# A retention-attention and gMLP kernel: per-chunk states formed for two chunks at once and summed in SBUF, four rotating PSUM banks, zero products in the head, a new order

## The chip, the cores and the metric

The kernel runs on one core of one Trainium2 chip. The metric is device time in microseconds (us) of the whole program: loads, arithmetic and stores. The core has a tensor engine (PE), a vector engine (DVE), a scalar engine (ACT), a general engine (POOL) and a queue engine (SP) that issues nearly all DMAs. Each of them works through its own list of instructions in order and waits on semaphores for the others.

## The reference

Inputs q, k, v have 8 batches, 8 heads, 576 positions and 64 elements in f32. A retention attention feeds a gated MLP that also mixes along the sequence:

```python
scores = scale * q @ k^T                       # per batch and head
ret    = scores * gamma[h] ** (s - t)          # 0 for t > s
x      = (ret @ v), heads side by side         # [8, 576, 512]
h      = gelu_tanh(x @ w_in)                   # [8, 576, 1024]
u, vv  = halves of h
v_n    = (vv - mean) / sqrt(var + 1e-6) * g_ln
v_s    = w_sg @ v_n + b_sg                     # along the 576 positions
out    = x + (u * v_s) @ w_out
```

## The kernel before

The 8 x 576 = 4608 positions are cut into 36 chunks of 128; two neighbouring chunks form a block, so there are 18 blocks of 256 positions. Nine chunks hold two batches, and the fifth chunk of each nine (index 4, called MID) holds the end of one batch and the start of the next.

Attention is done chunk by chunk: inside a chunk by masked scores, across chunks by a state, the running sum of k-transposed times v over all earlier chunks of the batch. The decay goes into factors on q and v, so the state is a plain sum. For block j the steps are: `ld` (loads q, k, v by SP), `cast` (to bf16, with the decay factors; on POOL, DVE or ACT), `T` and `Te` (PE transposes q and k, an engine copies the result to SBUF) or `Td` (a DMA transposes), `Sc` and `Sce` (scores of four heads, DVE multiplies by the mask), `Z` and `Ze` (state products of one chunk, copy of the state as bf16 `zb`), `inter` (state times q for one half), `intra` (masked scores times v, and the rest of the state products), `intrae` (copy of the attention to `xT`). The MLP follows with `V`, `Ve`, `mom`, `pow`, `cen`, `norm` (the v half of w_in, gelu, layer norm), `U`, `Ue` (the u half), `W`, `We` (w_sg along the sequence, times u) and `O`, `Oe`, `st` (w_out, copy, store). `wT` transposes w_sg once at the start.

The order of all these steps, and for many the engine (A, D or P for ACT, DVE, POOL) and the PSUM bank, is written out by hand in one string, `ORDER`. The program takes the words in turn, so the string sets each engine's list.

PSUM has eight banks. Tag `y` holds the scores (two banks), tag `z` the attention or V (two), `x0`, `x1` and `w` one bank each, which T, wT, U, W and O share in turn. The eighth bank belongs to the state alone: `Z` of every chunk adds into it, over a whole batch, and `Ze` reads it after each chunk:

```python
z = zcur[0]                                     # one bank, kept over the chunks of a batch
nc.tensor.matmul(z[half(r), kk, :], s["kb"][lo, a, kk, r, :], s["vb"][lo, a, h, :],
                 start=(first and r not in begun), stop=True, skip_group_check=True)
```

`Z` of chunk c uses the 64 rows of that chunk (32 for MID), so its 16 products lie on one half of PE's rows, on two column halves in turn.

Of the kernel before, what the change touches and what calls it, by code (L numbers as in the profile page):

```python
# [32 lines left out]
mom:3:1 ld:6:k:0 We:0:0:0 Z:5:0 Sce:5:0 Ze:5:0:A Ve:4:b W:0:3:0:2:w cast:6:q:P ld:7:q wc:out:A W:0:1:1:2:x1 ld:6:v:0 We:0:3:0 W:0:2:0:2:x0 We:0:2:0
inter:5 We:0:1:1 Sc:5:1 W:0:1:0:2:w W:0:2:1:2:x0 W:0:3:1:2:x1 Sce:5:1 We:0:2:1 We:0:1:0 intra:5 cast:6:k:P pow:2:1 Z:5:1 We:0:3:1 ld:7:k intrae:5:A
U:4:1:w T:6:q:x0 V:5:b:z cen:3:0 Ue:4:1 Ze:5:1:A cen:3:1 cast:7:q:P T:6:k:x1 mom:4:0 U:5:1:w ld:7:v Te:6:q:A W:0:0:1:0:x0 Te:6:k:A U:5:0:x1 Sc:6:0
norm:2:1:P cast:6:v:D mom:4:1 Z:6:0 Ve:5:b W:0:0:1:1 cast:7:k:P Ue:5:1 O:0:0:w We:0:0:1 Sce:6:0 mom:5:0 pow:3:b Ue:5:0 Ze:6:0:A O:1:1:x0 Z:6:1 inter:6
norm:3:0:D ld:8:q cast:7:v:P Td:7:q Oe:1:1:A Sc:6:1 Sce:6:1 ld:8:k Oe:0:0:A O:0:1:x0 norm:3:1:A T:7:k:x1 ld:8:v cen:4:1 mom:5:1 Ze:6:1:A Te:7:k:A
U:4:0:w bd:1 ld:9:q intra:6 Ue:4:0 Sc:7:0 pow:4:b intrae:6:A Z:7:0 Oe:0:1:A ld:9:k O:1:0:x1 cen:5:1 cen:4:0 ld:10:k Sce:7:0 V:6:b:z Ze:7:0:D
cast:8:k:A Ve:6:b cast:8:q:P pow:5:b Oe:1:0:A U:6:1:x0 norm:4:0:D T:8:k:w inter:7 Te:8:k:D Sc:7:1 cast:8:v:P Z:7:1 Sce:7:1 T:8:q:x1 Ue:6:1 cen:5:0
st:0 Ze:7:1:A W:1:3:0:2:w ld:9:v W:1:2:0:2:x0 Te:8:q:A We:1:2:0 intra:7 Sc:8:0 cast:9:k:P Z:8:0 norm:4:1:A Td:9:k W:1:0:1:2:x1 We:1:3:0 W:1:0:0:2:w  # L40
ld:11:k:0 W:1:1:0:2:x0 mom:6:0 We:1:0:1 norm:5:0:A We:1:0:0 intrae:7:A U:7:0:x1 Ue:7:0 V:7:b:z We:1:1:0 Ve:7:b O:2:1:x1 mom:6:1 cast:10:k:P ld:10:q
Oe:2:1:A Ze:8:0:D Sce:8:0 cast:9:q:P ld:11:q:0 mom:7:0 cast:9:v:P ld:10:v W:1:3:1:2:w inter:8 Sc:8:1 We:1:3:1 norm:5:1:P ld:11:q:1 Sce:8:1 mom:7:1
T:9:q:x1 U:6:0:w W:1:1:1:2:x0 We:1:1:1 Te:9:q:A Z:9:0 Ue:6:0 cen:6:1 cen:6:0 intra:8 intrae:8:A Sc:9:0 pow:6:b W:1:2:1:2:x1 norm:6:0:D cast:10:q:P
U:7:1:w V:8:b:z norm:6:1:A W:2:3:0:2:x0 pow:7:b Ue:7:1 Td:10:k We:1:2:1 Sce:9:0 ld:11:k:1 Ve:8:b Ze:9:0:A ld:11:v:1 cen:7:0 W:2:0:0:2:x1 U:8:1:w
cast:10:v:P We:2:3:0 Z:9:1 inter:9 Sc:9:1 Ue:8:1 mom:8:0 W:2:0:1:2:x0 T:10:q:w ld:13:k:1 We:2:0:0 Sce:9:1 norm:7:0:A Te:10:q:D W:2:3:1:2:x1 Ze:9:1:A
intra:9 st:1 Sc:10:0 Z:10:0 W:2:1:1:2:w We:2:3:1 We:2:0:1 Ze:10:0:A O:3:0:x1 intrae:9:A mom:8:1 cast:11:q:P ld:11:v:0 pow:8:b Sce:10:0 cast:11:k:A
We:2:1:1 cen:7:1 O:3:1:x0 V:9:b:z cen:8:1 Td:11:q U:8:0:w Oe:3:1:A Oe:3:0:A cen:8:0 Ve:9:b W:2:2:1:2:x1 norm:7:1:A mom:9:0 norm:8:0:P inter:10 Z:10:1
Sc:10:1 Ue:8:0 We:2:2:1 Ze:10:1:A O:2:0:x0 Oe:2:0:A W:2:2:0:2:x1 Sce:10:1 norm:8:1:P Td:11:k W:3:0:1:2:w W:2:1:0:2:x0 ld:12:q ld:13:q:0 intra:10
Sc:11:0 ld:12:k We:2:2:0 We:3:0:1 We:2:1:0 intrae:10:A st:3 ld:12:v cast:11:v:P Z:11:0 W:3:0:0:2:w W:3:3:0:2:x0 Sce:11:0 cast:12:q:P V:10:b:z We:3:0:0
cast:12:k:P Td:12:k W:3:2:0:2:w Ve:10:b We:3:3:0 ld:13:v:1 cast:12:v:P Ze:11:0:D U:9:0:x0 Ue:9:0 We:3:2:0 T:12:q:x1 Z:11:1 inter:11 Sc:11:1 Ze:11:1:A  # L50
mom:9:1 Te:12:q:D O:5:1:w ld:13:k:0 W:3:2:1:2:x1 pow:9:b Sce:11:1 We:3:2:1 U:10:1:x0 intra:11 Oe:5:1:A Z:12:0 cen:9:0 cen:9:1 Sc:12:0 Ue:10:1
intrae:11:A O:5:0:x0 mom:10:0 ld:13:q:1 cast:13:k:A norm:9:0:P Sce:12:0 Oe:5:0:A cast:13:q:P V:11:b:z ld:14:k mom:10:1 Ve:11:b W:3:1:0:2:x1 st:2
U:9:1:w Ze:12:0:A mom:11:0 Ue:9:1 pow:10:b Td:13:k We:3:1:0 O:4:0:x0 cen:10:0 inter:12 Sc:12:1 Oe:4:0:A norm:9:1:A Sce:12:1 U:11:1:w T:13:q:x1
cen:11:0 Te:13:q:A W:3:1:1:2:x0 intra:12 We:3:1:1 st:5 Z:12:1 ld:14:q cast:14:k:P Ue:11:1 Sc:13:0 mom:11:1 O:4:1:x1 U:11:0:w ld:15:k:1 cen:10:1
intrae:12:A U:10:0:x0 V:12:b:z Oe:4:1:A cast:14:q:D O:7:0:x1 pow:11:b ld:13:v:0 Ze:12:1:A ld:14:v Sce:13:0 Ue:11:0 ld:15:q:0 U:12:0:w Ue:10:0
norm:10:0:P Td:14:q U:12:1:x0 norm:10:1:D norm:11:0:A Ve:12:b Ue:12:0 cast:13:v:P W:4:2:1:2:w Oe:7:0:D Td:14:k ld:15:q:1 mom:12:0 cen:11:1 We:4:2:1
Ue:12:1 W:4:3:1:2:x1 We:4:3:1 inter:13 norm:11:1:P cast:14:v:P Z:13:1 Sc:13:1 W:4:2:0:2:w st:4 mom:12:1 W:4:0:1:2:x0 Ze:13:1:A ld:15:v:0 We:4:2:0
# [35 lines left out]
def kernel(  # L93
# [274 lines left out]
    def Z_mm(j, c):  # L368
# [4 lines left out]
        if first:  # L373
            zcur[0] = psZ.tile([128, KK, D], F32, name="zp")
# [229 lines left out]
```

## Time and profile before

| | |
|---|---|
| median of 3 runs | 219.21 us (219.15 to 220.51) |
| profiled execution | 218.48 us, span 216.7 us |
| PE busy | 194.7 us (90%) |
| DVE busy | 170.3 us (79%) |
| ACT busy | 123.3 us (57%) |
| POOL busy | 122.1 us (56%) |
| DMA | 48.47 MB, mean 224 GB/s |

The span is the time from the first to the last record of the profiled execution; what is missing to its own time, 1.78 us, lies around the span. Busy times are sums over the engine's records. A row of a timeline has start, length, engine, line, operation, tiles and count, and in brackets the idle time before it with what ended it. A group row of the page has count, busy time and mean of one in ns.

### The profile page before, as it was taken

The numbers are of one execution on the slowest core, as the hardware profiler recorded it, in microseconds if no ns is written. First come the engines' busy times: TensorE is split into PE (matmuls) and PEld (weight loads), VectorE is DVE, ScalarE is ACT, GpSimd is POOL, SyncE is SP. The second block draws the span as 40 slices with busy tenths as digits, with TensorE's granted clock in tenths as the row PEclk, the third lists the DMA queues.
The fourth block names the chain that finished last, engine by engine and source line by source line (L and its number), as shares of the span: only waits on it lengthen the run. The fifth ranks groups of instructions, "written<-read, shape, count | busy, mean of one in ns | idle before, by whom it ended". The sixth has DMA issues, their size and how long they took to land.

```text
span 216.7 us, 7228 instructions
## 1 busy us (share of the span) xinstructions
PE 194.7 (90%) x3101; PEld 136.8 (63%) x3130; DVE 170.3 (79%) x289; ACT 123.3 (57%) x179; POOL 122.1 (56%) x144
## 2 busy tenths in 40 slices
PE   0468788899999989999999999999999999999993
PEld 0355566577677657686667767686756675666751
DVE  3666858988995899799977678797988887977770
ACT  3356475697868578567563477833674457633102
POOL 5055338889169996988368565659729422151000
PEclk9999999999999999999999999999999999999999
DMA  6999999998999999999779899999899999450755
GB/s 168 290 343 355 222 233 263 208 226 190 290 217 254 208 247 324 197 249 174 184 172 282 180 263 252 217 207 254 128 269 230 265 238 271 141 149 3 191 198 194
DMA packets 86704, 48.47 MB, mean 224 GB/s; under 512 B 24528, under 2 KB 79824, under 8 KB 86672
## 3 DMA queue, kind: packets, MB, share of 16 engines
q1 hardware_dynamic: 86560, 48.00, 96.7%
q8 instruction: 24, 0.39, 0.8%
q14 instruction: 8, 0.07, 0.1%
q10 hardware_dynamic: 112, 0.00, 0.0%
HBM read 33.05 MB, written 9.44 MB: 196 GB/s over the span
## 4 chain that ended last, share of the span: by engine, by line
PE 63%; DVE 16%; DMA 12%; ACT 2%; issue 2%; SPq 1%; POOL 1%; DVEq 0%; ACTq 0%; POOLq 0%
PE wp L523 14%; PE op L535 12%; DMA vf<-in_v_dram 12%; PE hv L454 11%; PE hu L509 10%; PE ot L419 5%; DVE ret L360 5%; PE sc L350 3%; DVE vc L484 3%; PE zp L382 2%; DVE bst L468 2%; PE op L538 2%; DVE vn L500 2%; PE wtp L279 2%; PE tp L327 2%
## 5 line engine op out<-in xcount | busy, mean ns | idle before, releaser
L360 DVE TENSOR_TENSOR ret<-sc,mask 128x1024 bf16<-128x1024 f32 x36 | 43.8, 1216 | 5.8 <-PE sc L350 5.6
L302 POOL TENSOR_TENSOR qb<-qf,gq 128x512 bf16<-128x512 f32 x30 | 32.7, 1109 | 22.1 <-DMA qf<-in_q_dram 20.7
L523 PE MATMUL wp<-wT,vn 128*128 128x288 bf16 x256 | 40.8, 286 | 0.1
L509 PE MATMUL hu<-xT,w_in 128*128 128x256 bf16 x288 | 36.8, 273 | 0.0
L535 PE MATMUL op<-w_out,gT 128*128 128x512 bf16 x126 | 35.0, 380 | 1.2 <-issue 0.3
L528 DVE TENSOR_TENSOR gT<-wp,uT 128x288 bf16<-128x288 f32 x64 | 28.0, 449 | 9.8 <-PE wp L523 8.2
L454 PE MATMUL hv<-w_in,xT 128*128 128x512 bf16 x133 | 34.0, 382 | 1.6 <-ACT xT L137 0.8
L137 ACT CAST xT<-ot 128x1024 bf16<-128x1024 f32 x17 | 22.3, 1311 | 17.8 <-PE ot L419 17.7
L484 DVE SCALAR_TENSOR_TENSOR vc<-vg,mv,g_bc 128x512 f32<-128x512 f32 x36 | 31.5, 897 | 0.2
L514 ACT ACTIVATE uT<-hu 128x512 bf16<-128x512 f32 x36 | 21.3, 599 | 16.7 <-PE hu L509 16.4
L509 PEld LDWEIGHTS <-w_in 128*128 128x128 bf16 x288 | 27.1, 98 | 5.0
L523 PEld LDWEIGHTS <-vn 128*128 128x128 bf16 x256 | 24.6, 98 | 8.0 <-issue 0.4
L309 POOL TENSOR_TENSOR vb<-vf,gv 128x1024 bf16<-128x1024 f32 x13 | 25.1, 1934 | 7.2 <-DMA vf<-in_v_dram 5.5
L468 DVE BATCH_NORM_STATS2 bst<-vg 128x6 f32<-128x512 f32 x36 | 24.6, 683 | 4.5 <-ACT vg L461 4.5
L461 ACT ACTIVATE vg<-hv 128x1024 f32<-128x1024 f32 (+1 forms) x19 | 18.6, 980 | 13.2 <-PE hv L454 11.6
L500 POOL TENSOR_SCALAR vn<-vc,rs 128x512 bf16<-128x512 f32 x12 | 20.6, 1720 | 9.3 <-DVE vc L484 9.2
L454 PEld LDWEIGHTS <-xT 128*128 128x128 bf16 x144 | 13.5, 99 | 14.7 <-ACT xT L137 1.4
L137 ACT COPY ob<-op 128x512 f32<-128x512 f32 x20 | 11.5, 586 | 18.5 <-PE op L538 17.8
L477 POOL TENSOR_SCALAR rs<-mv 128x2 f32<-128x2 f32 (+1 forms) x19 | 8.1, 427 | 23.8 <-DVE mv L469 22.8
L535 PEld LDWEIGHTS <-gT 128*128 128x128 bf16 x144 | 12.9, 98 | 11.6
L523 PE MATMUL wp<-wT,vnm 128*128 128x288 bf16 x64 | 18.0, 287 | 0.3 <-DVE kT L137 0.3
L350 PE MATMUL sc<-qT,kT 64*64 64x128 bf16 x576 | 16.3, 223 | 0.8 <-DVE ret L360 0.6
(74 smaller groups left out, 283.2 us busy)
## 6 DMA issues: line engine op xcount, KB each, us to landing
out_dram<-ob SPq DMA_DIRECT2D x16, 512.0 KB, 4.6
kf<-in_k_dram SPq DMA_DIRECT2D x12, 512.0 KB, 7.6
qf<-in_q_dram SPq DMA_DIRECT2D x12, 512.0 KB, 6.6
vf<-in_v_dram SPq DMA_DIRECT2D x12, 512.0 KB, 8.1
gT<-in_moe_w_in_dram SPq DMA_DIRECT2D x2, 1024.0 KB, 9.5
qf<-in_q_dram SPq DMA_DIRECT2D x4, 384.0 KB, 8.2
kf<-in_k_dram SPq DMA_DIRECT2D x4, 384.0 KB, 8.3
vf<-in_v_dram SPq DMA_DIRECT2D x4, 384.0 KB, 8.5
```

What stands on the lines that cost most here:

```text
L137: (nc.scalar.copy if eng == "A" else ENG[eng].tensor_copy)(o, i)
L302: ENG[eng].tensor_tensor(s["qb"][:, a], paired(x)[:, a], g, op=Alu.mult)
L309: ENG[eng].tensor_tensor(s["vb"][:].rearrange("p a h d -> p h a d"), x[:], bc(gv, j), op=Alu.mult)
L360: nc.vector.tensor_tensor(s["ret"][:, :, 2 * g:2 * g + 2].rearrange("p r x a t -> p r x (a t)"), PS.pop(("Sc", j, g))[:].rearrange("p r x ...
L454: nc.tensor.matmul(hv[:, n], xT[:, (2 * j + t) % (2 * RING), kk, :], w_in[:, kk, F2:], start=(kk == 0), stop=(kk == KK - 1))
L468: nc.vector.bn_stats(bst[:], s["vg"][:, t])
L484: nc.vector.scalar_tensor_tensor(s["vc"][:, t], s["vg"][:, t], s["mv"][:, t, 0:1], g_bc[:], op0=Alu.subtract, op1=Alu.mult)
L500: ENG[eng].tensor_scalar(vn[:], vc[:, t], rs[:, t:t + 1], None, op0=Alu.mult)
L509: nc.tensor.matmul(hu[:, i, :], w_in[:, kk, 128 * c:128 * c + 128], xT[:, c0:c0 + 2, kk, :], start=(kk == 0), stop=(kk == KK - 1), skip_gr ...
L523: nc.tensor.matmul(PS["W", b, c, x][:], vns[t0 + j][e][:, 128 * c:128 * c + 128], wT[:, e, j, x * HS:(x + 1) * HS], start=(j == 0), stop=( ...
L528: nc.vector.tensor_tensor(gT[:, c, col:col + HS], PS.pop(("W", b, c, x))[:], uT[:, c, col:col + HS], op=Alu.mult)
L535: nc.tensor.matmul(op[:], gT[:, c, 128 * i:128 * i + 128], w_out[:, c, :], start=(c == 0), stop=(c == KK - 1 and not turn), skip_group_che ...
```

## The change

Five things change; the arithmetic of the rest, the layer norm among it, stays.

- `Z` of a block issues the products of both its chunks in one group, alternating between the two halves of PE's rows, each chunk into a bank of its own. Blocks with a MID chunk run the two chunks one after the other, and the last chunk of two batches needs no state. The state's own bank is gone; there are now four rotating banks, `x0`, `x1`, `w`, `v`, for Z too.
- `Ze` adds the bank to the running sum of the batch in SBUF, in f32 (DVE), or copies it where a batch starts. A new step `Zc` casts that sum to bf16 (19 on ACT, 10 on POOL, 3 on DVE).
- A step `fill` issues products of zeros (128 columns by 512) on PE: 32 of them in eleven places up to the first V group of block 1.
- The 64 last rows of w_sg are staged in the gT ring (`s5`) instead of a tile of their own, and some tables of the set-up share buffers with later tiles.
- `ORDER` is written anew. Block 2's loads and attention stand ahead of the loads of the u half of w_in and of w_sg; the transposes of w_sg stand after block 2; many casts and copies change engines.

```diff
-zcur = [None]
-def Z_mm(j, c):
...
-    if first:
-        zcur[0] = psZ.tile([128, KK, D], F32, name="zp")
...
+def opens(i):
+    return i % NT in (0, MID)
+
+def Z_mm(j, c, tag):
+    s = blk[j]
+    PS["Z", j, c] = ps2("zp", [128, KK, D], tag)
+    if c == 0 and (2 * j + 1) % NT != NT - 1:
+        return
+    for part in (False, True):
+        rows = [[], []]
+        for c in range(2):
+            if ("Z", j, c) not in PS or ((2 * j + c) % NT == MID) != part:
+                continue
+            lo = slice(64 * c + (32 if part else 0), 64 * c + 64)
+            for a in range(2):
+                for kk in range(KK):
+                    for r in range(2):
+                        rows[c].append((r, 64, lambda z=PS["Z", j, c], lo=lo, a=a, kk=kk, r=r: nc.tensor.matmul(
+                            z[half(r), kk, :], s["kb"][lo, a, kk, r, :], s["vb"][lo, a, hd(r, kk), :],
+                            start=(a == 0 and kk == 0), stop=True, skip_group_check=True)))
+        interleave(rows)
 
 def Z_out(j, c, eng):
-    zb = zbs[2 * j + c + 1] = w3.tile([128, KK, D], BF, name="zb")
-    move(eng, zb[:], PS.pop(("Z", j, c))[:])
+    i = 2 * j + c
+    sums[i] = w2.tile([128, KK, D], F32, name="zs")
+    z = PS.pop(("Z", j, c))
+    if opens(i):
+        move(eng, sums[i][:], z[:])
+    else:
+        nc.vector.tensor_tensor(sums[i][:], z[:], sums[i - 1][:], op=Alu.add)
+
+def Z_cast(j, c, eng):
+    i = 2 * j + c
+    zbs[i + 1] = w3.tile([128, KK, D], BF, name="zb")
+    move(eng, zbs[i + 1][:], sums[i][:])
...
+def fill(n, tag):
+    o = ps2("idle", [128, 4, 128], tag)
+    for _ in range(n):
+        nc.tensor.matmul(o[:], zeros[:], zeros[:].unsqueeze(1).to_broadcast([128, 4, 128]), start=True, stop=True,
+                         skip_group_check=True)
...
-    wst5 = consts.tile([64, S], F32, name="wst5")
+    ..., "s5": flat[:64, :S]}
```

Of the string, its first words:

```diff
-ld:0:k rl ld:0:q ld:0:v cast:0:k:D ld:1:k T:0:k:x1 ld:1:q mk:0 cast:0:q:D Te:0:k:A T:0:q:x1 cast:0:v:D Z:0:0 ...
+ld:0:q warm rl mk:0 ld:0:k ld:0:v cast:0:q:P fill:10:v T:0:q:v ld:1:q cast:0:k:P ld:1:k fill:2:w T:0:k:w ldw:v ...
```

What this makes of the engines' lists is shown at three places. First DVE at the start of block 0; before, it casts k (`kb`) and scales q (`qb`) itself:

```order
L137 CAST kb<-kf 128x512 x2
L246 TENSOR_SCALAR mask_136<-rel 128x256
L302 TENSOR_TENSOR qb<-qf,gq 128x512 x2
L309 TENSOR_TENSOR vb<-vf,gv 128x8x2x64
L246 TENSOR_SCALAR mask_137<-rel 128x256
L249 MEMSET mask_137 32x4x16
L360 TENSOR_TENSOR ret<-sc,mask_136 128x2x512
```

And of the change, where `zs` is the sum of the states in SBUF:

```order
L259 TENSOR_SCALAR mask_134<-rel 128x256
L322 TENSOR_TENSOR vb<-vf,gv 128x8x2x64
L259 TENSOR_SCALAR mask_136<-rel 128x256
L262 MEMSET mask_136 32x4x16
L140 COPY zs<-zp 128x256
L373 TENSOR_TENSOR ret<-sc,mask_134 128x2x512
```

The casts of k and q of block 0 have moved to POOL, and the copy of the first state now stands on DVE between v's scaling and the first masking (`ret`).

Second, PE at the state products of block 1. Before, with buffer numbers, at the first of them, behind the scores (`sc`):

```order
L350 LDWEIGHTS kT_335
L350 MATMUL sc_350<-qT_322,kT_335 64x128
L382 LDWEIGHTS kb_239
L382 MATMUL zp_181<-vb_369,kb_239 64x64
```

And of the change, behind the V group (`hv`):

```order
L477 LDWEIGHTS xT_87
L477 MATMUL hv_363<-w_in_85,xT_87 128x512
L398 LDWEIGHTS kb_344
L398 MATMUL zp_381<-vb_358,kb_344 64x64
L398 LDWEIGHTS kb_344
L398 MATMUL zp_384<-vb_358,kb_344 64x64
```

Before, all 16 products go on into `zp_181`, the one bank; now 32 products take the banks `zp_381` and `zp_384` in turn.

Third, DVE in the middle of the program, around block 5's and block 6's states. Of the change:

```order
L506 SCALAR_TENSOR_TENSOR vc<-vg,mv,g_bc 128x512
L550 TENSOR_TENSOR gT<-wp,uT 128x288 x2
L413 TENSOR_TENSOR zs<-zp,zs 128x256 x2
L373 TENSOR_TENSOR ret<-sc,mask_134 128x2x512
L550 TENSOR_TENSOR gT<-wp,uT 128x288
L373 TENSOR_TENSOR ret<-sc,mask_134 128x2x512
L322 TENSOR_TENSOR vb<-vf,gv 128x8x2x64
L506 SCALAR_TENSOR_TENSOR vc<-vg,mv,g_bc 128x512
L413 TENSOR_TENSOR zs<-zp,zs 128x256
```

The three additions into `zs` stand ahead of the masking of scores there; before, the states of these chunks were copied to `zb` by ACT and no row of DVE stood in their place.

160 lines of the change are left out of this document (75 added, 85 removed).

## Prediction

> **What bounds the kernel now.** I read the page first: engine shares, slices, the chain that ended last.
>
> ```profile
> PE 194.7 (90%) x3101; PEld 136.8 (63%) x3130; DVE 170.3 (79%) x289; ACT 123.3 (57%) x179; POOL 122.1 (56%) x144
> ...
> PE   0468788899999989999999999999999999999993
> ...
> PE 63%; DVE 16%; DMA 12%; ACT 2%; issue 2%; SPq 1%; POOL 1%; DVEq 0%; ACTq 0%; POOLq 0%
> ```
>
> PE carries 63% of the chain and its row of slices is full from the ninth slice on. Then I asked for busy time by stage, cut at the ends of the attention of blocks 1, 5 and 9 and at PE's last instruction.
>
> ```profile
> core 0: us, PE busy (x) PEld busy (x) DVE busy (x) ACT busy (x) POOL busy (x), PEclk, DMA share, GB/s
> 0.00:24.60 24.60, 11.80 (x256) 8.81 (x258) 14.57 (x30) 12.38 (x16) 9.11 (x32) 1.00 0.99 283
> 24.60:63.20 38.60, 36.06 (x663) 25.90 (x667) 33.16 (x57) 26.89 (x39) 26.11 (x28) 1.00 1.09 230
> 63.20:105.10 41.90, 40.03 (x707) 29.44 (x709) 37.37 (x56) 28.22 (x41) 35.77 (x37) 1.00 1.14 241
> 105.10:212.90 107.80, 106.64 (x1500) 72.64 (x1514) 85.24 (x150) 55.27 (x82) 51.12 (x48) 1.00 0.89 203
> 212.90:216.70 3.80, 0.14 (x3) 0.00 (x0) 0.00 (x0) 0.59 (x1) 0.00 (x0) 1.00 0.44 168
> ```
>
> PE is idle 12.80 us in the head (24.60 less 11.80), then 2.54, 1.87 and 1.16 us, and 3.80 us of tail. So a gain can come from three places: the head, the 5.57 us of gaps behind it, and the PE work itself. The vector engine (DVE) is second: 89% busy in the third window (37.37 of 41.90), with 4.53 us left.
>
> **Term 1, the head: -0.9 us.** These rows carry it.
>
> ```profile
> 7.70 1.21 PE L327 MATMUL tp<-ident,qb 128*128 128x128 bf16 x8 [1.11 <-DVE qb L302]
> ...
> 15.08 1.07 PE L419 MATMUL ot<-ret,vb 64*64 64x128 bf16 x32 [1.32 <-DVE ret L360]
> ...
> 23.85 0.64 PE L419 MATMUL ot<-ret,vb 64*64 64x128 bf16 x32 [1.32 <-DVE ret L360]
> ...
> 37.72 0.62 PE L327 MATMUL tp<-ident,kb 128*128 128x128 bf16 x8
> ```
>
> ```profile
> 9.45 1.22 DVE L309 TENSOR_TENSOR vb<-vf,gv 128x1024 bf16<-128x1024 f32 x1 [1.21 <-DMA vf<-in_v_dram]
> ...
> 13.80 1.22 DVE L360 TENSOR_TENSOR ret<-sc,mask 128x1024 bf16<-128x1024 f32 x1 [0.36 <-PE sc L350]
> 15.71 1.43 DVE L137 CAST w_in<-gT 128x2048 bf16<-128x2048 f32 x1 [0.68 <-DMA gT<-in_moe_w_in_dram]
> ...
> 18.82 1.22 DVE L309 TENSOR_TENSOR vb<-vf,gv 128x1024 bf16<-128x1024 f32 x1
> ```
>
> ```profile
> 11.67 1.14 ACT L137 CAST kb<-kf 128x512 bf16<-128x512 f32 x2
> ```
>
> ```profile
> 13.09 2.10 POOL L302 TENSOR_TENSOR qb<-qf,gq 128x512 bf16<-128x512 f32 x2 [8.69 <-DMA qf<-in_q_dram]
> ```
>
> Eight transposes take 1.21 us at 7.70 and 0.62 us at 37.72, and 32 products of `intra` 1.07 against 0.64: early PE work runs at about half pace, though the granted clock reads 1.00 throughout. The new head issues ten products of zeros before the first transpose and 22 more up to about 25 us, so I take the fast pace from about 6 us on. (The Trainium skill, "TensorE: Matmul & The Clock Gate", section "What's actually happening", says that PE starts at half clock and is released after about 3.4 us of sustained activity; by that rule the zeros bring the fast pace, and the two durations agree with it.)
>
> The walk through the new order: v of block 0 is third in the load queue as before, so its scaling ends at 10.67 again. Both state products (about 0.5) and the scores (0.33, rows further down) end by 11.5; DVE copies the first state (0.41) and masks from 11.65 to 12.85, not from 11.84; the second mask runs 13.25 to 14.45, not to 15.02. q of block 1 is now the fourth load, in the place of k, which had landed by 11.67, so POOL scales it until 13.8; PE transposes it until 14.1 and then runs three zero products (0.65 at 0.216 each) before `intra` 0 at 14.75. That is only 0.33 earlier than 15.08, but the group takes 0.6 instead of 1.28. The next gate is the v half of w_in, the sixth load in both, cast by 17.14; the V group then ends near 18.9. v of block 1 was scaled from 18.82, behind another DVE step; without that I put the load at about 18.0 (estimate). Two masks and three adds later `intra` 1 starts at 22.95, not 23.85. Bounds: +0.3 if zeros don't warm PE (the three cost 1.3 ahead of `intra` 0), -1.8 as twice the walk.
>
> **Term 2, 24.6 to 63.2 us: -1.0 us.** Block 2's loads (six DMAs, 1.5 MB) and its attention now stand ahead of the u half of w_in, w_sg and all ten transposes of w_sg. On DVE w_u is cast behind block 2's v scaling, at about 27.5 if I continue the walk (estimate), so U starts some 4 us later, but attention of block 2 fills PE. One wait is new on SP: the last 64 rows of w_sg use the stage of w_u and wait for that cast; block 4's loads queue behind it.
>
> ```profile
> 34.26 1.32 SPq L158 DMA_DIRECT2D qf<-in_q_dram  x2
> ```
>
> They were issued from 34.26 and would now go from about 29, so nobody is later. PE's idle time here is 2.54 us; both ends are 0 and -2.5, and I take two fifths.
>
> **Term 3, the state products: -0.8 us.**
>
> ```profile
> 38.27 0.44 PE L382 MATMUL zp<-vb,kb 64*64 64x64 bf16 x16
> 38.65 0.64 PE L419 MATMUL ot<-ret,vb 64*64 64x128 bf16 x32
> ...
> 131.77 0.39 PE L350 MATMUL sc<-qT,kT 64*64 64x128 bf16 x16
> 132.10 1.05 PE L509 MATMUL hu<-xT,w_in 128*128 128x256 bf16 x8
> ...
> 134.14 0.64 PE L419 MATMUL ot<-ret,vb 64*64 64x128 bf16 x32
> 134.61 0.28 PE L419 MATMUL ot<-qT,zb 64*64 64x128 bf16 x8
> 134.72 0.32 PE L382 MATMUL zp<-vb,kb 64*64 64x64 bf16 x10
> ...
> 135.30 1.04 PE L535 MATMUL op<-w_out,gT 128*128 128x512 bf16 x3
> ...
> 208.98 2.75 PE L535 MATMUL op<-w_out,gT 128*128 128x512 bf16 x12
> 211.57 0.39 PE L538 MATMUL op<-ident,xT 128*128 128x128 bf16 x4
> ```
>
> What counts is from one group's start to the next: a lone Z group takes 0.38 (38.27 to 38.65, 24 ns a product), scores 0.33 (131.77 to 132.10), Z and scores together 0.58 (134.72 to 135.30), so Z there adds 0.25. Two chunks cost 0.50 to 0.76. The new group alternates halves of the rows as `intra` does, which issues 32 products in 0.47 (134.14 to 134.61, 14.7 ns). At that pace the 32 cost 0.47, at 24 ns 0.77. Only ten blocks get the joint group: four hold a half chunk and run in two parts, four have one chunk. I take 0.55 less 0.47, ten times; bounds -2.9 and +2.7. (The last two rows give the 0.216 us of a wide product: 2.59 us for 12.)
>
> **Term 4, DVE in the middle: +0.4 us.**
>
> ```profile
> L137 DVE CAST zb<-zp x6: 390/413/419, 56.8 to 170.6; 128x256 bf16<-128x256 f32 x6
> ...
> L528 DVE TENSOR_TENSOR gT<-wp,uT x64: 424/448/459, 57.9 to 209.2; 128x288 bf16<-128x288 f32 x64
> ...
> L500 DVE TENSOR_SCALAR vn<-vc,rs x5: 478/1369/2147, 73.2 to 200.6; 128x512 bf16<-128x512 f32 x5
> ```
>
> ```profile
> 73.24 2.15 DVE L500 TENSOR_SCALAR vn<-vc,rs 128x512 bf16<-128x512 f32 x1 [0.51 <-POOL rs L478]
> 73.17 1.93 POOL L309 TENSOR_TENSOR vb<-vf,gv 128x1024 bf16<-128x1024 f32 x1
> ```
>
> ```profile
> L302 DVE TENSOR_TENSOR qb<-qf,gq 128x512 bf16<-128x512 f32 x6 | 3.9, 690 | 2.3 <-DMA qf<-in_q_dram 2.3
> ```
>
> No row shows the add of PSUM and SBUF in f32; it lies between the state cast (0.413) and gT (0.448), which also takes one input from each and never leaves 0.46. So 0.43: 27 state steps on DVE instead of six add 9.1 us, three casts 1.2, and six q scalings leave (-4.1). The other exchanges on DVE are of both signs and I put them at nothing. Of this +6 us, blocks 3 to 9 get eleven state steps and a cast where three stood: +3.9 us against 5.44 and 4.53 us of idle DVE in the two windows. That cover takes nearly all, hence +0.4; bounds 0 and +3.9. The 19 casts on ACT and ten on POOL go to engines idle over 40% of the span; the second step makes the state some 0.4 us later, but from block 3 on at least 2 us of other PE work stands between a block's Z and `inter`. Without it the price would be 0.4 a block.
>
> **Term 5, four rotating banks: -0.5 us.** Before, 167 groups shared three banks (56 each), now 199 share four (50 each), 11% fewer. The gaps behind 63.2 are 3.03 us (1.87 and 1.16); 11% of them is 0.3, and W may follow W more freely. Bounds 0 and -3.0. The tail keeps its products, copies and stores: nothing.
>
> **Sum** -0.9 -1.0 -0.8 +0.4 -0.5 = -2.8 on the profiled execution's 218.48 (the span of 216.7 and 1.78 around it): 215.7. The median of the runs, 219.21, lies 0.73 above that execution, so I state 216.4.
>
> **Rivals.**
>
> ```profile
> 44.37 8.66 DMA vf<-in_v_dram
> ...
> 57.22 10.71 DMA vf<-in_v_dram
> ...
> 67.95 1.55 DVE vb L309
> ```
>
> *Loads set the pace.* The chain runs from 44 to 68 us through two loads of v. If they land when they did, terms 1, 2 and 4 are given back and only the Z products and banks remain: -1.3, 217.9. For it: DVE waited for that load. Against: PE stayed 93% busy in that window.
>
> *DVE becomes the bound, slower.* While POOL worked on v, the DVE norm at 73.24 took 2.15 us, where its shortest took 0.48. POOL gets six more q scalings and ten casts. If DVE's idle 10 us of blocks 2 to 9 is forced by waits and stays, the 3.9 us land on the span, and stretched vector steps add about 0.8: -0.9 -0.8 +4.7 = +3.0, 222.2. It decides once DVE is over 95% busy between 33 and 98 us while PE idles more than 6 us there. Against: DVE is 86% and 89% busy in those two windows, so there is room.
>
> *The joint Z doesn't do what it says:* 32 products at the lone group's 24 ns cost 0.77, so term 3 is +2.2 and the time 219.4. The `intra` row speaks against it. (The Trainium skill, same page, section "Wait — 56ns, not 53.3ns?", states that starts of products never come closer than about 25 ns; by it the group costs 0.80. The trace disagrees: 14.7 ns.)
>
> *The gaps close:* term 2 at its far end and half of the 3.03 us of term 5, -0.9 -2.5 -0.8 -1.5 = -5.7: 213.5. For it: these gaps are waits for banks and casts, and Z no longer waits for its own read-out. Against: DVE, which must free more banks, is the fuller engine.
>
> **How the numbers follow.** Forecast 0.45 (216.4, own range 214.8 to 218.0), loads 0.18, DVE 0.15, slow Z 0.08, all gaps 0.14. About 1% (2.2 us) is what a measurement of this kernel can tell from no change. Faster by more than that: 0.32 of the forecast, 0.14 of the gaps, 0.04 of the loads: 0.50. Slower: 0.13 of DVE and 0.02 of Z: 0.15. The rest, 0.35, is no change. The range reaches from 212.5, a little beyond the gaps case, to 221.5, short of the DVE case's centre; outside are about 0.08 on each side.
>
> **What would show it.** Transposes at 7 us taking 0.6, `intra` 1 starting near 23.0; block 5's attention ending with less than 14 us of PE idle so far; groups of 32 state products 0.45 to 0.55 apart from the next group; adds of 0.43 us on DVE; PE idle under 3 us from 63 us to its last product. I am wrong if v loads land late behind the moved weights, if DVE holds the chain between 40 and 100 us, or if `inter` waits for the state.

## The result, and the profile after

The changed kernel takes 222.23 us (median of four executions, 221.00 to 223.47); the kernel before, run beside it, takes 219.67 (219.15 to 220.51). The ratio is 1.012, 95% interval 1.007 to 1.017: slower, where 216.4 was forecast, and 0.7 us beyond the end of the range. (The clock falls in some executions of either kernel; ratios here leave the most disturbed executions out, seven of twelve in e2 and in e6, and medians are over all.) The profiled execution took 223.43 us with a span of 221.7, so 5.0 us more span than before. From the page:

```profile
span 221.7 us, 7347 instructions
...
PE 205.7 (93%) x3162; PEld 136.6 (62%) x3162; DVE 176.3 (80%) x305; ACT 124.8 (56%) x185; POOL 121.2 (55%) x155
...
PEclk9799999999999999999999999799999999999998
...
q8 instruction: 25, 0.41, 0.9%
```

PE's busy time has grown by 11 us, but 11.6 us of it are the zeros (their group has 32 matmuls of 486 ns in the mean). New is the row of the granted clock, which was all nines before: it dips in the second slice (half clock from 8.3 to 11.7 us) and in the 26th, near 140 us. The same cuts as in the forecast, at the ends of the attention of blocks 1, 5 and 9 (to 0.1 us; block 5's last four products come behind its cut and end at 67.9) and at PE's last product:

```profile
0.00:23.10 23.10, 19.29 (x287) 9.41 (x287) 14.05 (x33) 10.76 (x14) 9.74 (x24) 0.93 1.06 251
23.10:67.20 44.10, 40.61 (x712) 28.50 (x704) 37.95 (x63) 30.00 (x45) 32.57 (x49) 1.00 1.11 252
67.20:103.30 36.10, 34.80 (x663) 24.72 (x662) 34.08 (x57) 27.68 (x42) 28.47 (x28) 1.00 1.06 229
103.30:217.00 113.70, 111.00 (x1527) 73.97 (x1516) 90.21 (x155) 56.00 (x87) 50.41 (x55) 0.98 0.95 200
```

By these cuts block 1 is done 1.5 us sooner (24.6 before), block 5 4.0 us later (63.2), with 49 more products ahead of it in the new order, block 9 again 1.8 us sooner (105.1), and PE's last product 4.1 us later (212.9). The loss is in the last row, where PE is idle 2.70 us (1.16 before) and the clock is below full. PE's timeline shows one place:

```profile
136.84 1.04 PE L531 MATMUL hu<-xT,w_in 128*128 128x256 bf16 x8
137.81 0.64 PE L442 MATMUL ot<-ret,vb 64*64 64x128 bf16 x32
138.28 0.22 PE L442 MATMUL ot<-qT,zb 64*64 64x128 bf16 x2
140.92 0.24 PE L442 MATMUL ot<-qT,zb 64*64 64x128 bf16 x2 [2.42 <-issue]
...
142.60 1.91 PE L531 MATMUL hu<-xT,w_in 128*128 128x256 bf16 x8
```

In the middle of one group PE stands for 2.42 us, and the profile names no engine and no transfer for it, only "issue". Behind it eight products of the same form take 1.91 in place of 1.04 us. A table of windows gives the granted clock there (the last but two of its columns):

```profile
138.00:141.40 3.40, 0.98 (x68) 0.85 (x59) 0.41 (x1) 0.20 (x1) 0.76 (x1) 1.00 1.26 210
141.40:144.90 3.50, 3.50 (x26) 2.25 (x16) 3.23 (x6) 3.13 (x5) 1.32 (x2) 0.51 0.66 131
144.90:150.00 5.10, 5.10 (x33) 2.77 (x30) 3.58 (x9) 2.16 (x4) 1.36 (x2) 1.00 0.99 239
```

Half clock for 3.5 us costs 1.7. With a second pause of this kind, 0.44 at 67.68, the three come to 4.6 of the 5.0 us. So there are two questions: what stops PE, and where the forecast's 2.8 us went besides.

### The profile page after: what moved, and what is told of

The parts are those of the page before. It is cut to its first block, busy times and chain, and to the rows that moved or that the text cites. A ratio compares the mean times of both kernels' runs of the same rounds, so it can differ in the third digit from the quotient of the medians.

```text
span 221.7 us, 7347 instructions
## 1 busy us (share of the span) xinstructions
PE 205.7 (93%) x3162; PEld 136.6 (62%) x3162; DVE 176.3 (80%) x305; ACT 124.8 (56%) x185; POOL 121.2 (55%) x155
## 4 chain that ended last, share of the span: by engine, by line
PE 61%; DMA 12%; SPq 10%; DVE 9%; POOL 3%; issue 2%; ACT 0%; POOLq 0%; DVEq 0%
PE wp L545 15%; PE op L557 15%; DMA qf<-in_q_dram 12%; PE hu L531 10%; PE hv L477 9%; SPq L161 8%; PE ot L442 5%; PE sc L363 3%; PE op L560 2%; SPq L218 2%; PE zp L398 2%; DVE ret L373 2%; POOL qb L315 2%; DVE vc L506 2%; DVE gT L550 2%
## 5 line engine op out<-in xcount | busy, mean ns | idle before, releaser
L315 POOL TENSOR_TENSOR qb<-qf,gq 128x512 bf16<-128x512 f32 x36 | 38.1, 1082 | 33.4 <-DMA qf<-in_q_dram 28.5
L531 PE MATMUL hu<-xT,w_in 128*128 128x256 bf16 x288 | 37.6, 277 | 0.1
L506 DVE SCALAR_TENSOR_TENSOR vc<-vg,mv,g_bc 128x512 f32<-128x512 f32 x36 | 35.3, 993 | 0.9 <-POOL vn L522 0.8
L557 PE MATMUL op<-w_out,gT 128*128 128x512 bf16 x144 | 35.9, 380 | 0.0
L140 ACT CAST xT<-ot 128x1024 bf16<-128x1024 f32 x15 | 19.7, 1311 | 19.9 <-PE ot L442 19.6
L545 PEld LDWEIGHTS <-vn 128*128 128x128 bf16 x256 | 24.6, 98 | 7.3 <-issue 0.5
L322 POOL TENSOR_TENSOR vb<-vf,gv 128x1024 bf16<-128x1024 f32 x12 | 23.2, 1933 | 10.2 <-DVE gT L550 7.2
L140 ACT COPY ob<-op 128x512 f32<-128x512 f32 x21 | 12.3, 585 | 16.3 <-PE op L560 16.0
L522 POOL TENSOR_SCALAR vn<-vc,rs 128x512 bf16<-128x512 f32 x9 | 14.5, 1612 | 6.2 <-DVE vc L506 6.0
L500 POOL TENSOR_SCALAR rs<-mv 128x2 f32<-128x2 f32 (+1 forms) x19 | 6.2, 325 | 21.3 <-DVE mv L492 15.7
L363 PE MATMUL sc<-qT,kT 64*64 64x128 bf16 x576 | 15.4, 220 | 0.9 <-DVE ret L373 0.8
```

The lines of the kernel that those rows point to most:

```text
L140: (nc.scalar.copy if eng == "A" else ENG[eng].tensor_copy)(o, i)
L315: ENG[eng].tensor_tensor(s["qb"][:, a], paired(x)[:, a], g, op=Alu.mult)
L322: ENG[eng].tensor_tensor(s["vb"][:].rearrange("p a h d -> p h a d"), x[:], bc(gv, j), op=Alu.mult)
L363: nc.tensor.matmul(o, s["kT"][half(r), a, kk, half(c)], s["qT"][half(r), :, kk, half(c)], start=True, stop=True, skip_group_check=True)))
L506: nc.vector.scalar_tensor_tensor(s["vc"][:, t], s["vg"][:, t], s["mv"][:, t, 0:1], g_bc[:], op0=Alu.subtract, op1=Alu.mult)
L531: nc.tensor.matmul(hu[:, i, :], w_in[:, kk, 128 * c:128 * c + 128], xT[:, c0:c0 + 2, kk, :], start=(kk == 0), stop=(kk == KK - 1), skip_gr ...
```

## Experiments: what stops PE

**Theory: late instructions.** The queue "q8 instruction" moves 25 packets of 16 KB for PE's 6,324 matmuls and weight loads, about 253 to a packet. The theory is that one comes late, behind loads. Between 128 and 138 us the transfers of the changed kernel are these, with no row of q8 at all; in the kernel before the same ten microseconds have one.

```profile
DMA packets 4835, 2.38 MB, mean 238 GB/s; under 512 B 1827, under 2 KB 4573, under 8 KB 4835
## 3 DMA queue, kind: packets, MB, share of 16 engines
q1 hardware_dynamic: 4835, 2.38, 118.3%
issues: line engine op xcount, KB each, median us to landing
```

The first run is the changed kernel again. Each group of runs from here on had a chip of its own, with the kernel before beside it (medians 219.4 to 219.8).

> The changed kernel as it is, for how often the pause comes and what it costs. In its first profile TensorE stands still for 2.42 us at 138.50 us, in the middle of block 13's intra products, for nothing that the profile names, and its granted clock is 0.83 from 140 to 150 us. Theory 'late instructions' (TensorE's own instruction packets, 16 KB each on the instruction queue, 25 of them for its 6,324 instructions, come late behind the loads): the pause stands at the same place again to within 1 us, 1.5 to 3 us long, in every execution; the cold clock behind it comes in some, and so the times have two levels, about 221.0 and 223.4. Rival 'the throttle alone' (the clock gate stops the engine now and then): the pause comes at another place or not at all, and the executions at 221.0 are those without it.

Measured: median 223.32 us (218.81 to 226.66) against 219.44 before; one of the six executions, at 218.81, is below the kernel before. The pause is there again at the same instruction in block 13, 1.34 us long at 142.4, and a second, larger loss that the first profile didn't have (below). Only one execution of a run is profiled, so whether the other five had the pause isn't known. Then the limits of the packets were shifted, with all else left alone:

```diff
-            nc.tensor.matmul(o[:], zeros[:], <512 columns>)
+            for lo, hi in ((0, 2), (2, 4)):          # e2; e3: 256, 128, 128; e4: four of 128
+                nc.tensor.matmul(o[:, lo:hi], zeros[:], <128 * (hi - lo) columns>)
```

> Each of the 32 matmuls of zeros of 512 columns is split in two of 256: 64 more TensorE instructions in the first 30 us at the same column count, nothing else. Theory 'late instructions': packets of about 253 instructions fall due 64 instructions earlier in the program, some 2 us at TensorE's pace here, so the packet that was late at 138.5 us is asked for before or after the burst of loads: the pause goes or falls under 1 us, the time is 218.5 to 221, granted clock 0.985 or more. Another pause may come elsewhere. Rival 'the place' (something that this point of the program waits for): pause of 2.4 us at 138.5 as before, time 221.0 to 223.5.

> Each matmul of zeros is split in three (256, 128 and 128 columns): 128 more TensorE instructions in the first 30 us, nothing else. 'Late instructions': the packet is due half a packet earlier, 4 to 5 us: no pause at 138.5 us, time 218.5 to 221. 'The place': 2.4 us at 138.5 again, 221.0 to 223.5.

> Each matmul of zeros is split in four of 128 columns: 192 more TensorE instructions in the first 30 us, nothing else; for the packets this is the same as 64 fewer. 'Late instructions': the packet is due a quarter of a packet later: the pause moves to about 64 instructions further on (140 to 141 us) or goes, time 218.5 to 223. 'The place': 2.4 us at 138.5 again, 221.0 to 223.5. Told apart by where the pause stands in the profile.

Measured: e2 221.8 us, ratio 1.0025 (0.998 to 1.007); e3 224.06, 1.018 (1.013 to 1.023); e4 226.33, 1.027 (1.021 to 1.033). One shift alone thus moves the time by 2%. e2 has no such pause (releaser "issue", over 0.3 us) anywhere. e4 has three, 0.69 to 1.06 us each, none of them at the old place; two of them:

```profile
130.90 0.30 PE L546 MATMUL wp<-wT,vnm 128*128 128x288 bf16 x1 [0.69 <-issue]
...
145.23 0.22 PE L399 MATMUL zp<-vb,kb 64*64 64x64 bf16 x2 [1.06 <-issue]
```

What they share is a count. If PE's records are counted from the start (a weight load and its matmul are two, a semaphore's is one), the pause of the changed kernel, of e1 and of e3 stands behind record 4,545, which is 17 x 256 + 193, though in e3 that is another instruction of the program; those of e4 stand behind 449, 4,289 and 4,801: 1, 16 and 18 times 256, and 193. The short pause of the changed kernel at 67.68 us stands behind 1,985, 7 x 256 + 193. So "the place" is out.

The packets' own times tie the two together. Between 138.2 and 139.5 us, inside the pause, the changed kernel has its 17th packet (138.23 to 139.41):

```profile
q8 instruction: 1, 0.02, 5.7%
```

PE goes on at 140.92, 1.5 us behind it. In all profiles together there are 21 such pauses of over 0.4 us, and each ends 1.3 to 1.9 us behind the landing of packet n where it stands behind record 256n + 193 (18 to the record; the other three, in traces that miss 28 or 29 records, 2 to 17 short of it). In the twelve profiles that miss none, PE never got to that record sooner than 1.2 us behind packet n. (The Trainium skill, "Runtime: NRT & Kernel Launch", section "Instruction fetch mechanics", says that instructions come in 16 KiB blocks of 256 and that crossing a block's limit is mostly hidden. The size agrees with the counts; here a crossing was not hidden and cost up to 2.4 us.)

That the loads delay the packet is shown by two kernels, one that leaves two loads out (and so computes wrong values for block 14) and one that moves two.

```diff
+            if part in "kq" and j == 14:              # e6: block 14 reads block 13's tiles
+                loaded[j, part] = loaded[13, part]
+                continue
```

> Block 14's q and k loads are left out (it reads block 13's tiles): 1 MB less of transfers is issued between 129.9 and 132.5 us, in front of the instruction packet that came late at 138.23 us. Theory 'late instructions': at 0.25 MB/us the packet comes some 4 us sooner, so no pause of over 0.3 us at TensorE's instruction 4545, and no packet asked for past 256n+100 between 125 and 150 us; time 2 to 4 us under the changed kernel's in profiles that are alike otherwise. Rival 'the place': the pause of 1.5 to 2.6 us in the middle of block 13's intra products stays.

Measured: 221.61 us, ratio 0.999 (0.994 to 1.003), profiled 219.42 with a span of 217.4. No pause from 105 us to the last product, and between 128 and 138 us:

```profile
q1 hardware_dynamic: 3675, 2.08, 97.3%
q8 instruction: 2, 0.03, 1.4%
```

e13 has all loads, and w_sg's casts later as in e5 below:

```diff
-ld:15:k:0 W:3:3:0:2:v ... Ze:13:1:A ld:14:q intrae:12:A ... Td:14:k
+W:3:3:0:2:v ... Ze:13:1:A intrae:12:A ... Td:14:k ld:14:q ld:15:k:0
```

> The kernel with w_sg's casts later, and two loads more put off: block 14's q and block 15's first k piece are issued behind block 14's k transposes (near 137 us) in place of 130 to 132.5 us; order alone, all loaded. 'Late instructions behind loads': 0.9 MB less stands in front of the packet that came at 138.2 us, it comes some 3 us sooner, and TensorE's pause of 1.3 to 2.4 us in block 13's intra products goes (under 0.4). The profile's span is 1.2 to 1.6 us under the one with w_sg's casts later alone (218.6, with a head of 3.4 us at half clock): 217.0 to 217.4, the median 219 to 221 against 222.6. Rival: the later q load makes block 14 late by the same 2 us, and the median stays at 222.

Measured: 226.16 us, ratio 1.016 (1.008 to 1.023). The pause in block 13 is gone (no idle time is reported there; two packets came between 128 and 138 us), so the first theory holds: the 17th packet begins 92 to 150 records ahead of record 4,545 in e6, e13 and e14 (below, with e13's order), which have no pause there, and 5 to 76 ahead in the five profiles of these loads in their old place (the changed kernel, e1, e5, e7, e8), which all have one. But the time is not the 219 to 221 that was expected. The rival's cost is there, and another packet came late in block 5:

```profile
69.12 0.25 PE L442 MATMUL ot<-qT,zb 64*64 64x128 bf16 x4 [1.80 <-issue]
...
150.82 0.43 PE L442 MATMUL ot<-qT,zb 64*64 64x128 bf16 x8 [2.49 <-DMA qT<-qb]
```

A mend of one pause only made others. The same came of joining e2's shift with e5's order:

> The changed kernel with both mends: w_sg's casts behind block 3's state, and the zeros in halves, which moves TensorE's packet limits by 64 instructions. If pauses and the cold clock behind them are what made the change slower, no pause of over 1.3 us stands between 30 and 205 us but for one near 168 us that the shifted kernel had (1.32 us behind an output), no fall of the clock behind 20 us in the profile, and the median falls by 2.5 to 5 us from the changed kernel's 223.3 to 218 to 220.5, about the time before (219.45) or up to 1.5 us under it. Rival 'the change has other costs': median over 221.

Measured: 222.75 us, ratio 1.016 (1.011 to 1.021). The pauses at 40 and 138 us are gone, and a new one of 1.70 us, again "issue", stands at 114.7, behind record 3,763; 28 records are missing in this trace, and 14 more would be 14 x 256 + 193.

## Experiments: what a pause does to the clock

In e1's profile the loss is in another place. The state of block 3 is cast on GpSimd (POOL) behind w_sg's first cast, which waits for its load, and PE's product with that state waits for POOL. The rows are PE's, POOL's, and windows:

```profile
41.62 0.31 PE L442 MATMUL ot<-qT,zb 64*64 64x128 bf16 x8 [1.64 <-POOL zb L140]
```

```profile
40.51 0.71 POOL L140 CAST uT<-gT 128x576 bf16<-128x576 f32 x1 [3.98 <-DMA gT<-in_moe_w_sg_dram]
41.18 0.40 POOL L140 CAST zb<-zs 128x256 bf16<-128x256 f32 x1
```

```profile
42.40:52.70 10.30, 9.82 (x90) 6.04 (x90) 4.54 (x7) 6.02 (x10) 8.94 (x12) 0.50 0.82 148
52.70:60.00 7.30, 7.30 (x129) 5.34 (x131) 5.73 (x10) 4.61 (x7) 5.10 (x4) 1.00 1.20 260
```

A wait of 1.64 us, with another of 0.73 close behind, is followed by 10.3 us at half clock: 5.1 us lost. e3 and e4 show the same near 41 us, e2 (1.43) and e8 (1.64) have the wait at full clock, and the first profile of the changed kernel has no such wait. e5 takes the cause away:

```diff
-Sc:3:0 sg:0:P Ze:3:0:D sg:1:A Zc:3:0:P ... sg:2:A ... sg:4:P V:2:0:x1 cen:1:0 inter:3 Ve:2:0 sg:3:P Sc:3:1 wT:5:w Sce:3:1 wT:1:x0 wT:3:x1 intra:3
+Sc:3:0 Ze:3:0:D Zc:3:0:P ... inter:3 Sc:3:1 V:2:0:x1 Sce:3:1 cen:1:0 sg:0:P sg:1:A sg:2:A sg:4:P sg:3:P Ve:2:0 intra:3 wT:5:w wT:1:x0 wT:3:x1
```

> The five casts of w_sg go behind the cast of block 3's state on GpSimd and behind the work of ScalarE's queue there, and one gate product of block 2 and block 3's intra products go ahead of w_sg's transposes on TensorE: order alone. In the profiles of the four kernels run so far on this chip, TensorE stands for 1.6 to 2.4 us near 40 us because block 3's state lies behind w_sg's first cast on GpSimd, which waits for its load, and in three of the four the granted clock falls to one half at 42 to 44 us for 6.8 to 10.2 us (3.4 to 5.1 us of work lost). Theory 'a pause of about 2 us, then half clock': no pause over 1.1 us between 36 and 46 us, no fall of the clock between 40 and 55 us, the median 2 to 4 us lower than the changed kernel's 223.3 on this chip (219.5 to 221.5). Rival 'the clock falls of itself': the falls stay, the median stays within 1 us of 223.3.

Measured: 222.62 us, ratio 1.011 (1.006 to 1.015), profiled 220.40. PE's longest wait there is 0.92, and the clock stays full from 39 to 60 us, as expected; the median came down by 0.7 only, where 2 to 4 were expected; the pause at 138 us stays (1.28). Its span of 218.6 less 1.28 for the pause is 217.3, that of e6. (The head ran 3.4 us at half clock in e5, as in the changed kernel, but block 1's attention ends at 23.0 all the same.) Over all profiles, the wait for block 3's state, 1.3 to 2.0 us, is in five of the nine with the changed kernel's order there (e1 to e4, e8) and in none of the four with e5's.

To see cause and effect alone, a pause was made in the kernel before:

```diff
+    def hold(n, tag):                                 # e9: n = 2, e10: n = 4
+        ...
+        nc.tensor.matmul(o[:], hz[:, :128], hz[:], start=True, stop=True)
+        for _ in range(n):
+            nc.scalar.copy(hz[:], o[:])
+        nc.tensor.matmul(o[:], hz[:, :128], hz[:], start=True, stop=True)
-We:2:3:1 We:2:0:1 Ze:10:0:A O:3:0:x1
+We:2:3:1 We:2:0:1 hold:n:x0 Ze:10:0:A O:3:0:x1
```

> The kernel before, with one made pause at a place where TensorE is otherwise busy and its clock full (between block 9's and block 10's attention, near 108 us): one matmul of zeros, two ScalarE copies of its 128x512 result (0.585 us each by the page's rows), and one matmul that reads them. TensorE should stand for some 1.3 to 1.8 us there. Theory 'a pause of about 2 us or more, then half clock for 3.4 us or a multiple': this one is too short, no fall of the clock within 6 us of it, time 1 to 2 us over before. Rival 'any pause does it': half clock for 3.4 us or more behind it, time 3 to 5 us over before.

> The same in the kernel before with four copies: TensorE should stand for 2.6 to 3.2 us near 108 us. Theory 'a pause of about 2 us or more, then half clock': the granted clock falls to one half some 3 us behind the start of the pause, for 3.4 us or a multiple, in this profile and in most executions: 2.5 to 3 us of pause and 1.7 to 5.1 us of lost clock, time 3.5 to 8 us over before. Rival 'the clock falls of itself, or only in the changed kernel': time 2.5 to 3 us over before and the clock at 1.00 behind the pause.

Measured: e9 221.41 us, ratio 1.008 (1.004 to 1.012); e10 223.12, 1.019 (1.013 to 1.026). First e9's windows, then e10's:

```profile
107.00:110.00 3.00, 2.21 (x17) 1.38 (x19) 2.43 (x5) 2.99 (x5) 0.54 (x2) 1.00 0.29 46
110.00:113.00 3.00, 3.00 (x23) 1.89 (x21) 0.05 (x1) 2.18 (x4) 3.00 (x3) 1.00 0.55 101
```

```profile
107.00:109.10 2.10, 0.10 (x1) 0.00 (x0) 2.10 (x4) 1.87 (x4) 0.89 (x2) 0.99 0.95 125
109.10:112.50 3.40, 2.47 (x9) 1.31 (x11) 1.16 (x2) 2.94 (x5) 2.07 (x2) 0.50 0.00 0
112.50:116.00 3.50, 3.50 (x24) 2.08 (x23) 0.00 (x0) 1.73 (x3) 2.95 (x2) 1.00 0.60 129
```

After 1.52 us of idle time (e9) the clock stays full; in e10's 2.93 us it falls 2.0 us after the stop and comes back 3.4 us later. In one of e10's four executions the mean clock was 1.00, so the fall is likely but not sure. A long wait isn't the only way to it: in e9's head, and in e15's (below), the clock fell at 36.6 and 37.5 us with no wait of over 0.6 us in the 3.4 us before, in which PE was busy for 77%. (The Trainium skill, "TensorE: Matmul & The Clock Gate", section "What's actually happening", has a free-running window of 3,413 ns, and half clock after at least one idle window. The lengths here, 3.4 us, twice and three times that, agree with the window; a whole idle window was not needed, 2 to 3 us of pause did it.)

## Experiments: where the forecast gain went

e7 asks whether loads set the pace of the head (it leaves four loads of v out, and so computes wrong values), e12 and e15 what the zeros bring, e8 what the joint state products bring, e14 what the waits for banks cost.

```diff
+            if part == "v" and 2 <= j <= 5:           # e7: these blocks read block 1's tile
+                loaded[j, part] = loaded[1, part]
+                continue
```

> The v loads of blocks 2 to 5 are left out (they read block 1's tile): 2 MB less to move, about 8 us of all queues at the 0.25 MB/us of the first 60 us, nothing else. Theory 'loads set the pace of the head' (by 32, 50 and 68 us both kernels have moved the same 8.5, 12.7 and 17.1 MB, so the head's gain is taken back when blocks 3 to 6 wait for their loads): GpSimd's waits for q between 20 and 70 us fall from some 18 us to under 8, block 5's intra ends at 62 to 64.5 us in place of 67.2, and what was gained stays to the end (2 to 4 us). Rival 'engines set the pace' (VectorE and GpSimd busy): block 5's intra stays within 1 us of 67.2.

Measured: 221.26 us, ratio 1.006 (1.004 to 1.009). POOL's waits for q between 20 and 70 us, 16.4 us in the changed kernel (its row of waits has sum, count and the longest), are gone; yet block 5's attention ends at 70.8 (67.9 in the changed kernel's first profile, 71.6 in e1). With loads out of the way, three engines meet: POOL scales q at 40.75 while VectorE (DVE) centres, DVE's step takes 2.77 us in place of 0.74, and PE waits 2.02 for the mask behind it, with half clock for 6.8 us after.

```profile
POOL qb L315 <- DMA qf<-in_q_dram: 16.4, 5, 9.1
```

```profile
40.75 2.07 POOL L318 TENSOR_TENSOR qb<-qf,gq 128x512 bf16<-128x512 f32 x2
```

```profile
40.71 2.77 DVE L509 SCALAR_TENSOR_TENSOR vc<-vg,mv,g_bc 128x512 f32<-128x512 f32 x1
43.41 1.21 DVE L376 TENSOR_TENSOR ret<-sc,mask 128x1024 bf16<-128x1024 f32 x1
```

The run is confounded by that pause: neither theory is shown by it.

The zeros were left out in e12 (fill returns at once) and added alone to the kernel before in e15 (fill:10:w ahead of T:0:k, fill:2:w behind it, fill:3:w ahead of Z:0:0):

> The changed kernel without the 32 matmuls of zeros (its psum tiles and all else as changed). Forecast, term 1: the zeros warm TensorE for the first products; without them block 0's first transposes take some 0.9 us in place of 0.4 and block 1's intra ends 0.9 us later (24.0 for 23.1). Rival 'loads set the head': block 1's intra ends within 0.3 us of 23.1. It has 64 TensorE instructions fewer, so a late packet may stand elsewhere, as with 192 more: only the first 30 us are compared.

> The kernel before with 15 matmuls of zeros in its head alone (10 ahead of block 0's first transposes, 2 behind them, 3 ahead of its first state products), its order else as it was. Term 1 alone: block 0's transposes take 0.4 in place of 0.9 us, block 0's and 1's intra end 0.3 to 0.9 us sooner, and since the head then waits for loads, 0 to 0.5 us of that is left at the end: 218.9 to 219.6 against 219.4. Rival 'the zeros were the gain': 1 us or more at the end, under 218.5.

Measured: e12, 225.73 in its one execution, takes 0.61 us for four of block 0's first transposes where the changed kernel takes 0.40, and block 1's `intra` ends at 25.4 in place of 23.2. In e15 block 1's `intra` ends at 23.2 where it ended at 24.6, but block 2's at 41.5, later than the 39.4 before, and the time is 219.96, ratio 0.998 (0.995 to 1.002). (Both profiles have half clock on the way, e12 from 23.1 us, under block 1's `intra`, and e15 for 3.4 us from 37.5, which costs 1.7 at block 2; e15 also has a late packet of 1.45 us, so the blocks say more than the times.) The zeros are worth some 1.4 us in the head, and nothing of it is left at the end.

```diff
-            rows = [[], []]
             for c in range(2):
+                rows = [[], []]
...
-            interleave(rows)
+                interleave(rows)
```

> The state products of a block's two chunks are issued one chunk after the other, not turn about; as many instructions, all else as changed. The forecast took 14.7 ns per product turn about (32 in 0.47 us) against 0.27 us per chunk of 16 before: 0.07 us a block over ten blocks, 0.7 to 0.8 us in all that this gives back. Theory 'the banks work at once': a group of 32 goes from about 0.45 to 0.54 us or more. Rival 'turn about buys nothing': 0.45 stays, to within 0.03. The time can't tell it: the two differ by under 1 us.

Measured: block 6's 32 products in the changed kernel, then in e8; each with the group behind it.

```profile
76.67 0.47 PE L398 MATMUL zp<-vb,kb 64*64 64x64 bf16 x32
77.07 1.04 PE L557 MATMUL op<-w_out,gT 128*128 128x512 bf16 x4
```

```profile
79.55 0.57 PE L398 MATMUL zp<-vb,kb 64*64 64x64 bf16 x32
80.05 0.82 PE L557 MATMUL op<-w_out,gT 128*128 128x512 bf16 x3
```

From start to start 0.40 against 0.50 us: turn about is 0.10 faster in this block, and 0.10 to 0.15 in three others. (e8's time, 224.25, has a late packet of 1.92 us in it and can't tell.)

e14, on e13's order, moves block 5's state products behind one gate group and onto free banks:

```diff
-W:0:2:0:2:x1 We:0:3:1 Zc:4:1:P Z:5:0:v ... Z:5:1:x0 We:0:2:0 ... Ze:5:1:D W:0:1:0:2:v ... T:6:k:x0 We:0:1:0
+W:0:2:0:2:x1 We:0:3:1 Zc:4:1:P W:0:1:0:2:v ... We:0:2:0 Z:5:0:x0 Z:5:1:x1 ... We:0:1:0 Ze:5:1:D ... T:6:k:v
```

> That kernel, and block 5's state products go behind one gate group and take banks that are free (x0 and x1), where the changed kernel's wait 0.7 us for VectorE's gate product on bank x0 and then 0.37 us for a state sum on bank v at 61 to 63 us. The four-bank term of the forecast (0.5 us gained) had the other sign there if these waits go and block 5's intra ends 0.7 to 1.1 us sooner; span 216 to 217 at a like clock. Rival: VectorE is what holds this stage, the wait comes back at the next product, block 5's intra within 0.3 us.

Measured: 224.44 us, ratio 1.018 (1.013 to 1.023). e13 itself has only the second of the two waits (0.38 for a state sum). It is gone in e14, but 0.28 for ACT's gelu and 0.59 for DVE's mask stand in its place at 63 to 66 us, and block 5's attention, a late packet in both included, ends at 70.4 against 69.4 in e13. Half of that 1.0 us was there at block 4's end, behind a late packet of 0.63 us at 21. So neither expectation came out: freeing the bank gained nothing, as the rival has it, but that DVE's queue limits the stage isn't shown.

## Why the prediction was wrong

The terms can be judged at full clock and without late packets in e6, whose profile is undisturbed (span 217.4, clock 1.00 in every slice). It is at the time before, 219.42 against 218.48 profiled and a ratio of 0.999, though it has 1 MB less to load; e2, which has all loads, has an undisturbed profile too (span 217.8) and a ratio of 1.003. So the change without these disturbances is worth nothing that can be measured, where 2.8 us of gain were forecast. With them it loses 2.5. e6's rows behind block 1:

```profile
23.60:67.90 44.30, 40.40 (x710) 28.28 (x704) 36.80 (x63) 29.59 (x45) 31.49 (x49) 1.00 1.10 250
67.90:104.50 36.60, 35.04 (x665) 24.64 (x660) 35.13 (x57) 27.89 (x42) 28.19 (x27) 1.00 1.08 222
104.50:213.40 108.90, 108.90 (x1531) 73.20 (x1519) 88.67 (x155) 55.71 (x86) 50.66 (x57) 1.00 0.94 199
```

PE is idle 5.46 us in them, as it was before (5.57): the 1.5 us of idle time that terms 2 and 5 counted on were not gained. PE's busy time in them is 1.6 us longer than before; as the trace before misses 29 products, it stays open how much of that is real, and so where the 0.8 us of term 3 went.

- **The step that failed first:** the sum had no term for PE's instruction packets or for the clock, because the kernel before has no pause over 1.1 us behind its head. They make 4.6 us in the profile after. The argument that block 4's loads "would now go from about 29, so nobody is later" looked at the issue of loads (they went from 32.0), not at what queues behind them; w_sg's own landing then held block 3's state (e1).
- **"If `inter` waits for the state"**, named as a way to be wrong, is what e1 to e4 and e8 show, by 1.3 to 2.0 us, though not the first profile. The step that failed is in term 4: the new casts on POOL were counted as busy time on an engine with room, not as instructions queued behind a load.
- **Term 1** was right: `intra` 1 starts at 22.46 (22.95 in the forecast, 22.94 in e6), and four of block 0's transposes take 0.40, the full pace. With the same zeros it ends between 23.0 and 24.3 in the profiles (24.6 before), so the gain is 0.3 to 1.6 us by execution.
- **Term 2** failed: it forecast 1.0 us less idle time between blocks 1 and 5; there are 3.49 us, against 2.54 (3.90 in e6).
- **Term 3**: joint products were forecast at 0.47, and they take 0.40, so 0.15 is gained a block by the forecast's own 0.55 for two lone groups; e8 shows 0.10 of it for turn about. The rival of the slow Z is out.
- **Term 4**: the add takes 0.417 (0.43 forecast). But DVE's centring step went from 897 to 993 ns in the mean, 3.8 us in all, by the mechanism that the DVE rival named: each of the 15 steps that took over 0.9 us lies beside a multiplication, a cast or a norm on POOL. That rival's condition (DVE over 95% busy between 33 and 98 us, PE idle over 6) was not met: 91%, with 2.2 us.

```profile
L506 DVE SCALAR_TENSOR_TENSOR vc<-vg,mv,g_bc 128x512 f32<-128x512 f32 x36 | 35.3, 993 | 0.9 <-POOL vn L522 0.8
...
L413 DVE TENSOR_TENSOR zs<-zp,zs 128x256 f32<-128x256 f32 x24 | 10.0, 417 | 5.4 <-PE zp L398 3.7 <-ACT zs L140 0.6 <-issue 0.3
```

- **Term 5** had the wrong sign at 61 to 63 us: two waits that the kernel before doesn't have, 0.72 for a bank that DVE must free and 0.37 for a state sum. The argument from 11% fewer groups a bank left out that Z now needs two banks at once; e14 couldn't show that this is what the first wait costs, since e13 doesn't have it.

```profile
61.73 0.44 PE L398 MATMUL zp<-vb,kb 64*64 64x64 bf16 x31 [0.72 <-DVE gT L550]
...
62.77 0.65 PE L545 MATMUL wp<-wT,vn 128*128 128x288 bf16 x4 [0.37 <-DVE zs L413]
```

- **The rival "loads set the pace"** (217.9) can't be called shown: POOL's waits for q grew from 20.7 to 28.5 us over the span, but e7, without 2 MB of loads, is at a ratio of 1.006 (1.004 to 1.009), not clear of the changed kernel's 1.012 (1.007 to 1.017), and has a pause of its own.

Open: which part of the order makes the loads crowd the packets more than in the kernel before. That kernel isn't free of it: e10, whose PE list up to 108 us is that of before, stands for 1.47 us at 42.9, 1.5 us behind its third packet, where the profile before has no pause. No version tried beats the kernel before; e2, e6 and e15 equal it. (The forecast's own sum for the gaps that close leaves out term 4's +0.4; with it that rival is 213.9.)

## What to carry to other kernels

Behind a PE that is 90% busy, look at the instruction queue's packets beside the loads: a burst of loads just ahead of a packet can stop PE for up to 2.4 us with no cause in the profile but "issue". Count such a stop twice, since 2 us or more of idle PE can bring 3.4 us or more at half clock. And price an instruction that is moved to a half idle engine by what stands ahead of it in that engine's queue, not by the engine's load.

## What the hardware showed that was not expected

- PE's pauses with releaser "issue" stand at 256n + 193 of its records in ten profiles, e15 with the order of before among them, 0.4 to 2.4 us each, and end 1.3 to 1.9 us behind the landing of the n-th packet of the instruction queue; the same program with its records shifted by 64 or by 192 takes 221.8 or 226.3 us.
- Six pauses of over 2.0 us (2.02 to 2.93) were each followed by half clock for 3.4 or 6.8 us in the profile (one of 2.00 in e3's head was not); of those between 1.3 and 2.0 us, from 25 us on, some were, for up to 10.3 us (e1, e3, e4, e14), and more were not (e2, e8, e9, e10, e11, e13, e15).
- DVE's step with two inputs from SBUF took 2.77 us beside a POOL multiplication, and 0.74 without. (The Trainium skill, "GPSIMD Engine Reference", section "1. Specifications", says that GpSimd shares its SBUF interfaces with VectorE; the trace agrees, with these numbers.)
